# Loading the 4 KB rows of wq ahead of its 24 KB rows in a decode attention kernel

## The chip, the cores and the metric

The kernel runs on one core of a Trainium2 chip (trn2). The metric is the device time of one execution in microseconds (us). All times quoted are medians of runs that were marked fast; each run of a changed kernel was compared with runs of the kernel before on the same chip. "Span" is the length of the profiled execution, about 2 us shorter than the measured time. In lines of the profile PE is TensorE, PEld its weight loads, DVE VectorE, ACT ScalarE, POOL GpSimd and SP SyncE; a q behind such a name means the part of the engine that issues, q1 is SyncE's DMA queue, and L226 is line 226 of the kernel. A packet is the piece that a DMA engine moves at a time, here one row of wq.

## The reference

One token goes through grouped attention over a cache of 65536 keys and values, and through a small token mixer; a gate mixes the two. The code is shortened.

```python
x = A_x                                              # 1 x 1 x 448, bf16
g = _sigmoid((x * gate_w).sum(-1, keepdims=True))
# attention: 16 query heads of 256, 8 key/value heads, cache of 65536
q = (x @ wq)                                         # wq: 448 x 4096
scores = einsum("bhqd,bhkd->bhqk", q, k) * (256 ** -0.5)
a = (softmax(scores) @ v) @ wo                       # wo: 4096 x 448
# mixer: layernorm of x, then gelu(h * w1 + b1) @ w2 + b2, w1 and w2 of 1792
return g * a + (1 - g) * b
```

K and V are 268 MB each, wq and wo 3.67 MB each.

## The kernel before

SyncE issues all large loads on one queue. The matrix wq has 448 rows. The first 384 go to `wq_a`, three rows to a partition, so each of the 128 partitions takes 24 KB that lie side by side in memory. The last 64 rows go to `wq_b`, half a row (4 KB) to a partition. Both lie in the buffer `vbuf` that the V blocks use later, so the first V block may be loaded only when q has been computed.

```python
wq_a = early[:, 0:WF * NQ].rearrange("p (j n) -> p j n", j=WF)     # WF = 3, NQ = 4096; early is vbuf
wq_b = early[:, WF * NQ:WF * NQ + HALF]                            # HALF = 2048
...
@block.sync
def _(eng):
    eng.dma_start(wq_a.rearrange("p j n -> p (j n)"),
                  A_wq[0:WF * P, :].rearrange("(p j) n -> p (j n)", p=P)).then_inc(sem_wq, 16)
    eng.dma_start(wq_b, A_wq[WF * P:DM, :].rearrange("r (a n) -> (r a) n", a=2)
                  ).then_inc(sem_wq, 16)
    ...
    for j in range(NP):                          # 32 blocks of 8 MB of K and of V
        if j >= 1:
            eng.wait_ge(sem_tr[NB - 1], BODY * (j - 1) + DC)   # half of block j-1 transposed
        if j == 0:
            load(kring, A_k_cache, j, HV, NV, 0, sem_k)        # half a block: rows of 32 KB
            load(kring, A_k_cache, j, 0, HV, 0, sem_kb)
        ...
        if j == 0:
            eng.wait_ge(s_q, 1)                  # q is there, wq is used up
            eng.wait_ge(s_hb, 1)
        else:
            eng.wait_ge(sem_pv, j)               # V block j-1 is used up
        load(vbuf, A_v_cache, j, ...)            # rows of 64 KB
```

ScalarE issues the row x and five small loads besides (gate, w1, b1, w2, b2); TensorE waits for them, then for both loads of wq:

```python
pe.wait_ge(sem_misc, 16 * 5)
pe.matmul(acc[:, WF + 2:WF + 2 + 3 * FT], wrows_b, identb, ...).then_inc(s_col, 1)
pe.wait_ge(s_xcol, 1)            # VectorE has copied the columns of x out of acc
pe.wait_ge(sem_wq, 32)           # both loads of wq
# 128 matmuls of q: 3 from wq_a and 1 from wq_b for each column
```

The softmax here doesn't subtract the row's maximum and nothing guards it: scores larger than these inputs give would overflow.

## Time and profile before

| kernel before | |
|---|---|
| measured time | 1266.03 us (1266.0 to 1266.64, 3 runs) |
| profiled span | 1264.0 us |
| DMA bytes, mean rate | 544.39 MB, 431 GB/s |
| share of SyncE's queue (q1) | 99.7% |
| busiest compute engine | PE, 73% |
| last wq row landed / q started | 12.1 us / 12.59 us |
| first V block issued | 17.54 us |

Read it from the DMA side: 544 MB must be moved, SyncE's queue alone takes 99.7% of what the 16 DMA engines could give in the span, and no compute engine is busy more than 73% of it. The lines of the profile that carry this stand in the prediction below.

### The profile page before, as it was taken

The page shows a single profiled execution, that of the slowest core. Times are in us where ns is not written, and L with a number is a line of the kernel's source. Part 1 is how long each engine was busy: PE and PEld are TensorE (multiplying, and loading weights), DVE is VectorE, ACT ScalarE, POOL GpSimd, SP SyncE. Part 2 cuts the span into 40 slices and gives each one's busy share as a digit, 9 for nine tenths or more (in the row PEclk, how much of TensorE's full clock was granted, in tenths as well). Part 3 has the DMA queues.
Part 4 walks back from the last instruction along what each step waited for, and adds up shares of the span by engine and source line. Part 5 has one row for each costly group of instructions (what it writes and reads, how often), then busy time and mean ns, then how long its engine had stood idle before and what let it go on. Part 6 is the DMA issues. An engine that isn't in the chain of part 4 may idle for free.

```text
span 1264.0 us, 38850 instructions
## 1 busy us (share of the span) xinstructions
PE 917.0 (73%) x17114; PEld 868.4 (69%) x17114; DVE 422.5 (33%) x764; ACT 538.2 (43%) x788; POOL 0.9 (0%) x7
## 2 busy tenths in 40 slices
PE   3876678766778667786676876758767688676688
PEld 2766668766677666786666876658766578666687
DVE  2433344333444333443222332323322233332233
ACT  1443345533355433454333553335533355433455
POOL 0000000000000000000000000000000000000000
PEclk9887788787898887987888987889887888877999
DMA  9999999999999999999999999999999999999998
GB/s 411 428 434 436 433 431 431 431 438 431 433 433 433 433 431 438 425 433 440 431 436 429 431 431 433 440 433 433 431 431 431 438 436 433 431 433 431 431 427 367
DMA packets 11623, 544.39 MB, mean 431 GB/s; under 512 B 1369, under 2 KB 1628, under 8 KB 2908
## 3 DMA queue, kind: packets, MB, share of 16 engines
q1 hardware_dynamic: 11522, 544.22, 99.7%
q8 instruction: 8, 0.13, 0.0%
q10 hardware_dynamic: 90, 0.01, 0.0%
q14 instruction: 3, 0.02, 0.0%
HBM read 544.22 MB, written 0.00 MB: 431 GB/s over the span
## 4 chain that ended last, share of the span: by engine, by line
DMA 70%; PE 29%; issue 1%; SPq 0%; DVEq 0%; DVE 0%; ACT 0%; ACTq 0%
DMA kring<-in_A_k_cache_dram 68%; PE kst L298 24%; PE sps L318 4%; DMA wo_sb<-in_A_wo_dram 2%; PE acc L358 0%; SPq L231 0%; SPq L265 0%; SPq L228 0%; SPq L226 0%; PE prj L405 0%; PE acc L347 0%; DVEq L92 0%; DVE out_row L634 0%; ACT pT L658 0%; ACTq L658 0%
## 5 line engine op out<-in xcount | busy, mean ns | idle before, releaser
L298 PE MATMUL kst<-ident,kring 128*128 128x128 f32 x4096 | 563.7, 299 | 304.9 <-DMA kring<-in_A_k_cache_dram 294.1
L669 ACT ACTIVATE ktT<-kst 128x1024 bf16<-128x1024 bf16 x512 | 500.0, 1021 | 667.3 <-PE kst L298 666.5
L298 PEld LDWEIGHTS kst<-ident,kring 128*128 128x128 f32 x4096 | 514.0, 156 | 314.8 <-issue 312.2
L569 DVE COPY ktT<-kst 128x1024 bf16<-128x1024 bf16 x512 | 354.2, 692 | 765.0 <-PE kst L298 742.0
L318 PEld LDWEIGHTS sps<-qcur,ktT 128*128 128x128 bf16 x8192 | 237.8, 96 | 4.1 <-issue 1.6
L318 PE MATMUL sps<-qcur,ktT 128*128 128x2 bf16 x8192 | 236.6, 163 | 1.3 <-issue 1.3
L358 PE MATMUL acc<-vbuf,pT 128*2 128x256 bf16 x4080 | 140.4, 305 | 3.8 <-issue 3.3
L358 PEld LDWEIGHTS acc<-vbuf,pT 128*2 128x2 bf16 x4080 | 105.2, 93 | 30.6 <-issue 3.8
L658 ACT ACTIVATE pT<-sps 128x32 f32 x256 | 51.8, 202 | 16.4 <-PE sps L318 16.4
L347 PE MATMUL acc<-pT,ones_sq 128*128 128x32 bf16 x256 | 11.7, 178 | 12.3 <-ACT pT L658 12.3
L347 PEld LDWEIGHTS acc<-pT,ones_sq 128*128 128x128 bf16 x256 | 8.6, 96 | 15.2 <-ACT pT L658 14.9
L675 ACT ACTIVATE z_b<-z_b 128x448 bf16<-128x448 bf16 x14 | 8.1, 577 | 20.5 <-DVE z_b L556 20.4
L575 DVE COPY accs<-acc 128x288 f32<-128x288 f32 x8 | 3.7, 458 | 38.5 <-PE acc L358 38.5
L394 PEld LDWEIGHTS acc<-sel,accs 128*64 128x64 f32 x112 | 10.8, 214 | 0.9
L394 PE MATMUL acc<-sel,accs 128*64 128x1 f32 x112 | 11.4, 260 | 0.0
L431 PE MATMUL acc<-vbuf 42*128 42x42 bf16 x1 | 0.2, 214 | 8.3 <-DMA b_b<-in_B_b_dram 8.3
L405 PE MATMUL prj<-wo_sb,oTn 128*1 128x112 bf16 x128 | 3.7, 244 | 3.1 <-DVE oTn L600 2.9
L431 PEld LDWEIGHTS acc<-vbuf 42*128 42x128 bf16 x1 | 0.1, 102 | 8.4 <-DMA b_b<-in_B_b_dram 8.4
L562 DVE TENSOR_TENSOR gu<-wtmp,z_b 128x448 bf16<-128x448 bf16 x14 | 5.5, 393 | 1.0
L554 DVE TENSOR_TENSOR z_b<-u_b,wtmp 128x448 bf16<-128x448 bf16 x14 | 5.5, 393 | 1.0
L550 DVE TENSOR_TENSOR z_b<-wtmp,u_b 128x448 bf16<-128x448 bf16 x14 | 5.5, 393 | 1.0
L548 DVE TENSOR_TENSOR wtmp<-u_b 128x448 bf16<-128x448 bf16 x14 | 5.5, 392 | 1.1
(89 smaller groups left out, 82.5 us busy)
## 6 DMA issues: line engine op xcount, KB each, us to landing
kring<-in_A_k_cache_dram SPq DMA_DIRECT2D x4, 4096.0 KB, 24.3
vbuf<-in_A_v_cache_dram SPq DMA_DIRECT2D x1, 6144.0 KB, 25.7
wo_sb<-in_A_wo_dram SPq DMA_DIRECT2D x7, 448.0 KB, 27.6
vbuf<-in_A_wq_dram SPq DMA_DIRECT2D x1, 3072.0 KB, 10.2
vbuf<-in_A_v_cache_dram SPq DMA_DIRECT2D x1, 1024.0 KB, 27.8
vbuf<-in_A_v_cache_dram SPq DMA_DIRECT2D x1, 768.0 KB, 28.9
vbuf<-in_A_wq_dram SPq DMA_DIRECT2D x1, 512.0 KB, 10.9
vbuf<-in_A_v_cache_dram SPq DMA_DIRECT2D x31, 29.7
```

Source lines behind the costliest of these rows:

```text
L298: ins = pe.transpose(kst[:, b, i * P:(i + 1) * P], kring_f[:, at + NT * (k % DC) + 4 * b + i, :], ident[:, :])
L318: ins = pe.matmul(sps[:, par, 2 * nt:2 * nt + 2], ktT[:, par, b, ntl * DH + dj:(ntl + 1) * DH:2], qcur[:, dj, :], start=(dj == 0), stop=(d ...
L347: pe.matmul(acc[:, DENC:SELC], ones_sq[:, :], pT[:, r, :], start=False, stop=(r == BODY - 1), skip_group_check=True)
L358: ins = pe.matmul(acc[o:o + REP, 0:DH], pT[:, r, 2 * nt:2 * nt + 2], vbuf[:, n, :], start=False, stop=False, skip_group_check=True)
L394: ins = pe.matmul(dst[hh * HP:(hh + 1) * HP, i:i + 1], accs[:, i:DH:2 * REP], sel[:, hh:hh + 1], start=False, stop=True, skip_group_check= ...
L548: vec.tensor_tensor(W, U, U, op=ALU.mult)
L550: vec.tensor_tensor(Z, W, U, op=ALU.mult)
L554: vec.tensor_tensor(Z, U, W, op=ALU.add)
L569: vec.tensor_copy(ktT[:, k % KTB, b, :], kst_b[:, b, :]).then_inc(sem_ev[b], 1)
L658: act.activation(pT[:, bass.ds(p0 + k % DC, 1), :].rearrange("p o n -> p (o n)"), sps[:, k % 2, 0:2 * NT], AF.Exp, scale=scale).then_inc(s ...
L669: act.activation(ktT[:, k % KTB, b, :], kst_b[:, b, :], AF.Copy).then_inc(sem_ev[b], 1)
L675: act.activation(z_b[:, :], z_b[:, :], AF.Tanh).then_inc(s_tanh, 1)
```

## The change

The intent is to have the short rows ahead of the long ones. Two issues on SyncE change places; nothing else does.

```diff
         def _(eng):
+            eng.dma_start(wq_b, A_wq[WF * P:DM, :].rearrange("r (a n) -> (r a) n", a=2)
+                          ).then_inc(sem_wq, 16)
             eng.dma_start(wq_a.rearrange("p j n -> p (j n)"),
                           A_wq[0:WF * P, :].rearrange("(p j) n -> p (j n)", p=P)).then_inc(sem_wq, 16)
-            eng.dma_start(wq_b, A_wq[WF * P:DM, :].rearrange("r (a n) -> (r a) n", a=2)
-                          ).then_inc(sem_wq, 16)
```

## The prediction

> **What bounds the kernel now.** I read the page first, for the busy shares and the DMA lines:
>
> ```profile
> PE 917.0 (73%) x17114; PEld 868.4 (69%) x17114; DVE 422.5 (33%) x764; ACT 538.2 (43%) x788; POOL 0.9 (0%) x7
> DMA  9999999999999999999999999999999999999998
> GB/s 411 428 434 436 433 431 431 431 438 431 433 433 433 433 431 438 425 433 440 431 436 429 431 431 433 440 433 433 431 431 431 438 436 433 431 433 431 431 427 367
> q1 hardware_dynamic: 11522, 544.22, 99.7%
> HBM read 544.22 MB, written 0.00 MB: 431 GB/s over the span
> ```
>
> No compute engine is busy more than 73% of the span. The DMA row stands at 9 in all slices but the last, and the one queue that SyncE feeds, q1, fills 99.7% of what 16 engines could do. The bytes are all needed: K and V are 8 x 65536 x 256 x 2 bytes = 268.4 MB each, wq and wo 448 x 4096 x 2 = 3.67 MB each, together 544.2 MB, as the page counts. A table of windows gives 433 GB/s from 60 to 1200 us. 544.22 MB / 433 GB/s is 1256.8 us of the span of 1264.0, so 7.2 us are left for the start, the landing of the last bytes and the tail.
>
> The end comes next. The chain of waits from 1180 us on names the last link:
>
> ```profile
> 1232.11 29.33 DMA wo_sb<-in_A_wo_dram
> 1261.44 0.04 issue
> 1261.49 0.39 PE prj L405 x6
> 1261.87 0.02 issue
> 1261.90 0.26 DVE out_row L634
> 1262.16 0.30 DVEq L92
> ```
>
> The last load of wo is issued at 1232.11 and lands 29.33 us later although it is 0.23 MB: it stands in the queue behind the last piece of V. After it come 2.56 us of projection, copy and store. So the time is: first byte, plus all bytes at the queue's rate, plus a fixed tail, provided the queue never runs dry. (The measured 1266.03 us are about 2 us over the profiled span; I take that as constant.)
>
> Now the place that the change touches. The timeline of the first 40 us, SyncE's rows:
>
> ```profile
> 0.74 0.41 SPq L226 DMA_DIRECT2D vbuf<-in_A_wq_dram  x1
> 1.20 0.41 SPq L228 DMA_DIRECT2D vbuf<-in_A_wq_dram  x1
> 1.67 1.10 SPq L231 DMA_DIRECT2D kring<-in_A_k_cache_dram  x2
> ...
> 17.54 0.33 SPq L231 DMA_DIRECT2D vbuf<-in_A_v_cache_dram  x1
> 17.91 0.43 SPq L260 DMA_DIRECT2D wo_sb<-in_A_wo_dram  x1
> 38.79 0.33 SPq L231 DMA_DIRECT2D kring<-in_A_k_cache_dram  x1
> ```
>
> Both loads of wq are issued back to back, and both halves of the first K block directly behind. SyncE then waits until 17.54 us before it may issue the first V block, which overwrites the buffer that holds wq: it needs q. The timeline also tells what q needs (start, duration, instruction, then in brackets what ended the idle time):
>
> ```profile
> 11.08 0.21 PE L431 MATMUL acc<-vbuf 42*128 42x42 bf16 x1 [8.33 <-DMA b_b<-in_B_b_dram]
> 12.37 0.17 DVE L517 CAST xcol<-acc 128x5 bf16<-128x5 f32 x1
> 12.59 0.24 PE L441 MATMUL sps<-xcol,vbuf 128*128 128x1 bf16 x3 [1.30 <-DVE xcol L517]
> ```
>
> and the list of DMA issues gives the landing of each load of wq, in us from its issue, as the last column:
>
> ```profile
> vbuf<-in_A_wq_dram SPq DMA_DIRECT2D x1, 3072.0 KB, 10.2
> vbuf<-in_A_wq_dram SPq DMA_DIRECT2D x1, 512.0 KB, 10.9
> ```
>
> The 24 KB rows land at 0.74 + 10.2 = 10.9 us, the 4 KB rows at 1.20 + 10.9 = 12.1. TensorE starts q at 12.59, and what released it is not wq but xcol. That copy waits for a matmul which waited until 11.08 for the five small loads (gate, w1, b1, w2, b2) that ScalarE issues.
>
> **What the Trainium skill says.** "DMA: Bandwidth & Descriptors", section "Queues, rings and completion order": on each engine descriptors are consumed in ring order. The trace agrees: the second load of wq lands 12.1 - 10.9 = 1.2 us after the first, and its 0.524 MB at 431 GB/s are 1.22 us. The same page, "Why a DMA increments its semaphore by 16 and not by 1", says that only the full 16 of a load means its data are there. Here both loads count on one semaphore and TensorE waits for 32, the sum of the two, so their order gives no early start to any consumer. Its section "Where 436 GB/s comes from" puts the ceiling of the 16 ports at 435.2 GB/s; 433 in the middle of this trace is 99.5% of it, so no order of rows can raise the rate by more than half a per cent. "Issuing engines are not separate DMA queues" says that loads issued by ScalarE run on the same 16 engines and interleave with SyncE's: the last small load is issued at 2.79 us and its release is seen only at 11.05, some 8.3 us, when wq is nearly through. The trace agrees in that they share.
>
> **The change part by part.** Nothing is removed or added. The orders of all instructions on TensorE, VectorE, ScalarE and GpSimd are the same; on SyncE the first two DMA issues change places. Rows, sizes, destinations and semaphores stay.
>
> The issue: 0.41 us each (the timeline: 0.74 and 1.20), so K is issued at 1.67 as before. Cost 0.
>
> The landing: 24 KB rows, 3.146 MB / 431 GB/s = 7.30 us. Landing 10.2 us after issue, they show about 2.9 us of start, completion and sharing. The 4 KB rows, now first, should land at about 0.74 + 2.9 + 1.2 = 4.8 us (an estimate from these durations) instead of 12.1. The 24 KB rows move behind them, from 10.9 to about 12.1. The later of the two, which is what the wait for 32 sees, stays at 12.1. Gain 0.
>
> The small loads: with shorter packets in front when they enter, they may land earlier than 11.05. Then q starts when wq is there, at 12.1 rather than 12.59: at most 0.5 us, which moves the V issue from 17.54 to about 17.05. If they land later, V goes later by as much.
>
> What half a microsecond at the V issue is worth: wq and the first K block are 3.67 + 8.39 = 12.06 MB, 28.0 us at 431 GB/s; the first bytes move at about 1.75 us, so the queue holds work until about 29.7 us. V issued at 17.54 has 12.2 us to spare. The next link has slack too: the second K block is issued at 38.79, and with V (8.39 MB, 19.5 us) and wo (0.46 MB, 1.1 us) the queue lasts until 29.7 + 20.6 = 50.3, so 11.5 us to spare. In the steady part, one K block was issued at 629.43 while the V block issued at 607.67 needed, at the median of 29.7 us, until 637.4: 8 us. A shift of 0.5 us in any of these stays hidden. Sum: 0 + 0 + 0, from 1266.03 to about 1266.
>
> **The rivals.** (1) The swap brings q forward and the gain reaches the end. For it: q stands at the head of the chain that frees the V buffer. Against it: the slack of 12.2 us behind it. Even if it went through undiminished, it would be 0.5 us, 1265.5. (2) The small loads are starved instead: their turn comes after more of the queue. For it: they already take 8.3 us. They could be 12.2 us later without cost. Should they come only after the whole first K block, near 30 us, then by the 6.5 us that now lie between 11.05 and the V issue, V would be issued near 36.5, the queue would be dry for about 7 us, and the time 1273, still within 0.6%. (3) The first load runs out before the second is ready, as it is now only 0.524 MB. Its bytes last 1.22 us; the second issue follows 0.46 us behind. A gap, if any, is some tenths: 1266.3. (4) TensorE bounds the steady part, its clock being granted at 0.84; then nothing at the start matters either. SyncE's 643.4 us of waits on the transposes look like this, but they are spent with the queue full, as the 99.7% shows. Again 1266.
>
> **Range and chances.** All paths but (2) lie within 1 us of 1266.0. The three runs before span 0.64 us, and another session may differ by about as much again, so the range is 1265.0 to 1267.2, with 1266.1 as the value. A gain of 2% would be 25 us, three times all that the kernel spends beyond its bytes (7.2 us of span); I give it 0.005. A loss of 2% needs a dry queue of 25 us, more than three times rival (2): 0.01.
>
> **What would show it.** In the changed profile the load of 512 KB lands about 4 us after its issue and that of 3072 KB about 11 us after its own, both near 4.8 and 12.1 us of the span; q starts between 12.1 and 12.8; V is issued between 17 and 18; q1 stays at 99.7%; the last load of wo lands within 1 us of 1261.4. The prediction is wrong if the V issue falls after 29 us, if the DMA row shows a slice below 9 ahead of the end, or if the middle rate leaves 433 GB/s by more than 1: each GB/s there is 2.9 us.

## The result, and the profile after

The changed kernel took 1265.59 us (1265.48 to 1267.19, 6 runs), the kernel before 1266.1 us (1265.96 to 1266.64, 6 runs). The ratio is 0.9997, with a 95% interval of 0.9984 to 1.001: the same, by the criterion of 2%. (A ratio here is the mean time of one kernel's fast runs over that of the other's of the same rounds, so it is not quite the ratio of the medians.) Still, five of the six new runs lie between 1265.48 and 1265.69, below every run of before (the sixth, 1267.19, lies above them all). So a second question is worth asking: are about 0.5 us really gained, and where?

The page of the changed kernel first; the queue is as full, and the bytes are the same:

```profile
DMA  9999999999999999999999999999999999999998
q1 hardware_dynamic: 11522, 544.22, 99.7%
HBM read 544.22 MB, written 0.00 MB: 431 GB/s over the span
```

The windows table gives 433 GB/s from 60 to 1200 us, as before. Next the list of DMA issues of the changed kernel (last column: us from issue to landing), then two lines of its timeline (start, duration, instruction, and in brackets what ended the idle time before it):

```profile
vbuf<-in_A_wq_dram SPq DMA_DIRECT2D x1, 3072.0 KB, 10.3
vbuf<-in_A_wq_dram SPq DMA_DIRECT2D x1, 512.0 KB, 3.4
```

```profile
11.54 0.21 PE L431 MATMUL acc<-vbuf 42*128 42x42 bf16 x1 [8.79 <-DMA b_b<-in_B_b_dram]
13.05 0.24 PE L441 MATMUL sps<-xcol,vbuf 128*128 128x1 bf16 x3 [1.30 <-DVE xcol L517]
...
18.00 0.33 SPq L231 DMA_DIRECT2D vbuf<-in_A_v_cache_dram  x1
```

The 4 KB rows land at 0.74 + 3.4 = 4.1 us and the 24 KB rows at 1.20 + 10.3 = 11.5, so wq is complete 0.6 us sooner than the 12.1 of before. But q starts later, at 13.05 instead of 12.59, because the small loads release TensorE at 11.54 instead of 11.08; V is issued at 18.00 instead of 17.54. Whatever was gained was not gained through q.

Then the chain of waits, which follows the K loads (start, duration in us). Before:

```profile
1.67 21.40 DMA kring<-in_A_k_cache_dram
...
38.79 34.06 DMA kring<-in_A_k_cache_dram
```

After:

```profile
1.67 21.05 DMA kring<-in_A_k_cache_dram
...
38.84 33.48 DMA kring<-in_A_k_cache_dram
...
1232.02 28.92 DMA wo_sb<-in_A_wo_dram
```

The first half of K lands at 22.72 instead of 23.07 us, the second K block at 72.32 instead of 72.85, the last load of wo at 1260.94 instead of 1261.44. The lead is 0.35, then 0.53, then 0.50 us: most of it is there when the first half of K has landed, and from the second K block on it stays. The step from 0.35 to 0.53 is not placed by these lines. The packets show the start as well. In the window from 1.5 to 3.3 us of the kernel before, the queue's line reads

```profile
q1 hardware_dynamic: 16, 0.39, 91.5%
```

that is, 16 packets (the first of each engine) took 0.915 x 1.8 us x 16 / 16 = 1.65 us each, while from 4.4 to 9 us a 24 KB packet takes 0.91 us by the same reckoning. So the first packet of each engine costs about 0.7 us more than a later one. After the change the same window holds

```profile
q1 hardware_dynamic: 113, 0.46, 76.2%
```

113 packets of 0.19 us, some seven for each engine, where a 4 KB packet in mid-stream takes 0.16 us (the same reckoning in a window of the run e2_k_half_first): about 0.25 us too much in all.

### The profile page after: what moved, and what is told of

It reads as the page before. It is cut to its first block, busy times and chain, and to the rows that moved or that the text cites. A ratio compares the mean times of both kernels' runs of the same rounds, so it can differ in the third digit from the quotient of the medians.

```text
span 1263.4 us, 38848 instructions
## 1 busy us (share of the span) xinstructions
PE 917.3 (73%) x17112; PEld 867.5 (69%) x17114; DVE 422.4 (33%) x764; ACT 537.9 (43%) x788; POOL 0.9 (0%) x7
## 3 DMA queue, kind: packets, MB, share of 16 engines
q1 hardware_dynamic: 11522, 544.22, 99.7%
## 4 chain that ended last, share of the span: by engine, by line
DMA 70%; PE 29%; issue 1%; SPq 0%; DVEq 0%; DVE 0%; ACT 0%; ACTq 0%
DMA kring<-in_A_k_cache_dram 68%; PE kst L298 24%; PE sps L318 4%; DMA wo_sb<-in_A_wo_dram 2%; PE acc L358 0%; SPq L231 0%; SPq L265 0%; SPq L228 0%; SPq L226 0%; PE acc L347 0%; DVEq L92 0%; PE prj L405 0%; DVE out_row L634 0%; ACT pT L658 0%; ACTq L658 0%
## 5 line engine op out<-in xcount | busy, mean ns | idle before, releaser
L347 PE MATMUL acc<-pT,ones_sq 128*128 128x32 bf16 x256 | 11.6, 178 | 12.2 <-ACT pT L658 12.2
## 6 DMA issues: line engine op xcount, KB each, us to landing
vbuf<-in_A_wq_dram SPq DMA_DIRECT2D x1, 3072.0 KB, 10.3
```

Of the source, the lines that this page charges most:

```text
L347: pe.matmul(acc[:, DENC:SELC], ones_sq[:, :], pT[:, r, :], start=False, stop=(r == BODY - 1), skip_group_check=True)
```

## The experiments

Twelve kernels ran, in three groups of four. The median of before was 1266.15 us in the first group (9 runs), 1266.0 in the second (9) and 1266.23 in the third (9). First the theories. In all of them, "the start" is the time until the DMA engines move data at their full pace. A: the 4 KB packets themselves make the start quicker. B: short rows cost less in front than between longer rows. C: the small loads of ScalarE share the engines differently. N: it is noise. D, formed after the first two groups: what counts is how the rows of the first load lie in memory, with their starts close together (4 or 8 KB apart) or 24 KB apart. In the kernel before they lie side by side too, but as each is 24 KB long, their starts are 24 KB apart. Beside D, A is called A2 below (only the length of the first packets counts), and L is a rival by which the address of the first load counts.

### Is the gain real?

e1_after_again is the changed kernel once more.

> The changed kernel once more, to see whether its 0.5 us are there at all. Theory A (the first packet of each DMA engine is 4 KB instead of 24 KB, so the engines get going sooner, and all later landings move forward by a constant): 0.4 to 0.6 us below the kernel before, with the last load of wo landing about 0.5 us earlier. Rival N (noise, nothing moved): the difference is under 0.2 us or changes sign between rounds.

Measured: 1265.6 us (1265.44 to 1265.97, 5 runs), 0.55 below before; the last wo landed at 1261.01 us, 0.4 earlier. Three of the five runs lie below all nine of before, the other two (1265.84 and 1265.97) below eight of them. The gain is there, at 0.04% of the time. (The 95% interval for the ratio, 0.9982 to 1.001, is too wide to tell it from 1; the claim rests on the order of the runs, on its return in a second set of runs, and on the landings.)

### Is it the length of the first packets, or the place of the short rows?

e2_k_half_first puts rows of 32 KB in front:

```diff
+            load(kring, A_k_cache, 0, HV, NV, 0, sem_k)     # then wq_a, wq_b, other half of K
```

> The first half of the first K block (rows of 32 KB) goes ahead of both loads of wq, which keep the order of before. Theory A: the first packet is 8 KB longer than before, so 0.1 to 0.3 us over the kernel before. Rival B (4 KB rows between 24 KB and 32 KB rows cost time, the start does not matter): equal to before within 0.1 us, since the 4 KB rows still stand between larger ones. Both: q comes about 9.7 us later, V is issued near 27.3 us, still ahead of the end of the queue near 29.7, so nothing else is lost.

Measured: 1268.04 us (1267.38 to 1269.44), 1.9 us over before, which neither theory allowed for. The loss lies elsewhere (below). The start itself speaks against A: wq was complete at 1.67 + 19.7 = 21.4 us, while the order of before would give about 12.1 + 4.19 MB / 431 GB/s = 21.8 with a half of K added. In e5 below, whose 24 KB rows come first and which has moved the same bytes by then, wq was complete at 1.67 + 20.4 = 22.1.

e3_three_8k loads the 24 KB rows as three loads of 8 KB rows that lie 24 KB apart:

```diff
+            wq_r = A_wq[0:WF * P, :].rearrange("(p j) n -> p (j n)", p=P)
+            for i in range(WF):
+                eng.dma_start(wq_a.rearrange("p j n -> p (j n)")[:, i * NQ:(i + 1) * NQ],
+                              wq_r[:, i * NQ:(i + 1) * NQ]).then_inc(sem_wq, 16)
-            pe.wait_ge(sem_wq, 32)
+            pe.wait_ge(sem_wq, 64)
```

> The 24 KB rows are loaded as three loads of 8 KB rows, then the 4 KB rows last, as before. Theory A: the first packet is 8 KB, so about 0.4 us below before (16/20 of 0.5), less what two more loads cost (their issue of 0.4 us each lies behind 1.05 MB of queued work, so about nothing). Rival B: no gain, 0 to 0.4 us over before, since there are more short rows between longer ones.

Measured: 1266.04 us (1265.79 to 1266.2), 0.1 below before, where A gave 0.4. This run shows something else of use. Its small loads landed much sooner, and V was issued 0.5 us earlier than before (timeline):

```profile
8.47 0.38 DVE L513 TENSOR_TENSOR vbuf<-vbuf 1x448 bf16<-1x448 bf16 x1 [2.51 <-DMA b_b<-in_B_b_dram]
...
17.04 0.33 SPq L233 DMA_DIRECT2D vbuf<-in_A_v_cache_dram  x1
```

An earlier V issue by itself therefore bought at most 0.1 us. That is the prediction's rival 1, tried.

e4_4k_of_24k_first loads the first 4 KB of each 24 KB row, then the other 20 KB, then the 4 KB rows of the remainder:

```diff
+            for n0, n1 in ((0, HALF), (HALF, WF * NQ)):
+                eng.dma_start(wq_a.rearrange("p j n -> p (j n)")[:, n0:n1],
+                              wq_r[:, n0:n1]).then_inc(sem_wq, 16)
```

> The first 4 KB of each 24 KB row are loaded first, then the other 20 KB, then the 4 KB rows of the remainder last, as before. Theory A: as the changed kernel, 0.4 to 0.6 us below before, although the 4 KB rows of the remainder stand where they stood. Rival B: equal to before within 0.1 us.

Measured: 1266.17 us (1266.11 to 1266.52), equal to before. Theory A falls: short packets in front are not enough. B, which had named this result, still stood.

### How much slack is there behind q?

Both runs leave the 24 KB rows first and move the issue of `wq_b`: in e5_4k_between_k between the halves of the first K block, in e6_4k_after_k behind both.

```diff
             if j == 0:
                 load(kring, A_k_cache, j, HV, NV, 0, sem_k)
+                eng.dma_start(wq_b, ...).then_inc(sem_wq, 16)      # e5
                 load(kring, A_k_cache, j, 0, HV, 0, sem_kb)
+                eng.dma_start(wq_b, ...).then_inc(sem_wq, 16)      # e6, in place of the other
```

> The 4 KB rows are loaded between the two halves of the first K block, to measure the slack that the prediction worked out. wq is complete only near 24 us, q some 5 us before V can be issued, so V is issued near 29. Slack theory (queue lasts until about 29.7 us): between 1266.0 and 1267.5 us, as the first byte of V comes about 1 us after its issue. Rival (slack much smaller than worked out, a late V costs at once): 5 us or more over before.

> The 4 KB rows are loaded after both halves of the first K block: wq is complete near 32 us, V issued near 37 us, while the queue ends near 31 us. Slack theory: the queue is dry for 6 to 8 us, and that comes out whole at the end, 1272 to 1274 us. Rival (the loss is made up later, as TensorE has time to spare): under 1269 us.

Measured: e5 1269.37 us (1268.24 to 1270.56), 3.4 over before; e6 1275.94 us (1275.56 to 1277.76), 9.9 over. V was issued at 27.12 and 36.67 us. In e6 the direction of the slack theory held, though 1275.94 lies above the 1272 to 1274 it named. The windows table has 360 GB/s from 25 to 31 us and 118 from 31 to 40; against 433 that is about 1.0 + 6.5 = 7.5 us missed, and nothing was made up later. A second, smaller gap comes at the second V block (issued at 78.41): 410 and 395 GB/s from 70 to 80 and from 80 to 90 us, another 1.4 us. In e5 the theory failed, as it had in e2 (and the rival's 5 us or more did not come either): V came well ahead of the end of the queue, and yet time was lost. The timeline and the windows table show where (its columns are the window, its length, the busy time of PE, PEld, DVE, ACT and POOL, the granted clock, the DMA share and GB/s). First e5:

```profile
49.36 0.33 SPq L229 DMA_DIRECT2D kring<-in_A_k_cache_dram  x1
73.95 0.33 SPq L229 DMA_DIRECT2D vbuf<-in_A_v_cache_dram  x1
```

```profile
70.00:80.00 10.00, 9.13 (x148) 7.25 (x141) 2.77 (x4) 3.82 (x5) 0.00 (x0) 0.82 0.64 246
```

and before:

```profile
63.58 0.33 SPq L231 DMA_DIRECT2D vbuf<-in_A_v_cache_dram  x1
```

```profile
70.00:80.00 10.00, 7.03 (x71) 7.02 (x72) 2.82 (x5) 4.08 (x5) 0.00 (x0) 0.66 1.01 434
```

In the windows lines, look at the last figure: 246 GB/s in e5 against 434 in before, for the same ten microseconds. The load that comes too late is the second V block, not the first. It waits for TensorE to have used up the first block (`sem_pv`), and TensorE could begin on that block only after q. It was issued at 73.95 us, 10.4 us later than in before, when the second K block was about to land (49.36 + 25.48 = 74.84). The dry stretch is 10 us x (1 - 246/433) = 4.3 us, and the span of this run is 1268.3 - 1264.0 = 4.3 us longer. In e2 the second V block came at 70.92, 7.3 us later than in before, and the span is 1.9 us longer. On the line through these two points the loss starts when the second V block is issued about 5 us late. That is an estimate, from two runs, and a rough one: without any loss this issue came at 60.84 us in the changed kernel and at 63.58 in before.

### Do the small loads make the difference?

In both twins ScalarE issues the small loads only after wq has landed; e7_before_small_late has the order of before, e8_after_small_late that of after.

```diff
+            act.wait_ge(sem_wq, 32)
             act.dma_start(grow_b, gate_w.rearrange("(a n) -> a n", a=1)).then_inc(sem_misc, 16)
```

> Order of before, but ScalarE issues its five small loads only when wq has landed, so their 88 packets no longer interleave with those of wq. Theory A: the start is as before, wq lands near 12 us, the time is that of before within 0.2 us as long as V is issued ahead of about 29 us. Rival C (the gain of the change came from the small packets, which shared the engines with 24 KB packets in another way): 0.3 to 0.6 us below before, or no difference left between this run and its twin with the order of after.

> Order of after, with the five small loads held back until wq has landed, as in the twin run with the order of before. Theory A: 0.4 to 0.6 us below the twin. Rival C: within 0.1 us of the twin.

Measured: e7 1272.64 us (1271.45 to 1275.35), e8 1272.07 us (1271.2 to 1274.35). Both are 6 us over before, because behind K's 32 KB rows the small loads took far longer than I had allowed for. In the chain of e7 they are the link

```profile
13.52 12.74 DMA b_b<-in_B_b_dram
```

and V was issued only at 32.76. The medians of the twins differ by 0.57 us, as A said and C did not; but the runs of each spread over 3 us, so this alone is weak. Firmer is the landing of wq, ahead of any of the five small loads; in the chains of e7 and e8 it is

```profile
1.20 10.82 DMA vbuf<-in_A_wq_dram
```

```profile
1.20 10.30 DMA vbuf<-in_A_wq_dram
```

that is, 12.0 us in e7 and 11.5 in e8. The 0.5 us are there without the small loads. C falls.

### Is it how the rows of the first load lie in memory?

Two twins of the changed kernel differ from it only in what the first load reads (the result is then wrong; sizes, counts and order stay). In e10_after_pitch_24k the 4 KB rows lie 24 KB apart; in e12_after_first_rows they lie side by side, but at the start of wq instead of its end.

```diff
+            eng.dma_start(wq_b, wq_r[:, 0:HALF]).then_inc(sem_wq, 16)                      # e10
+            eng.dma_start(wq_b, A_wq[0:DM - WF * P, :].rearrange("r (a n) -> (r a) n", a=2)
+                          ).then_inc(sem_wq, 16)                                           # e12
-            eng.dma_start(wq_b, A_wq[WF * P:DM, :].rearrange("r (a n) -> (r a) n", a=2)
-                          ).then_inc(sem_wq, 16)
```

> The changed kernel with the same sizes, counts and order, but the 4 KB rows are read from the first 4 KB of each 24 KB row, so 24 KB apart; the result is wrong on purpose. Theory D: the gain is gone, 1266.0 to 1266.3 beside 1266.1 of before. Theory A2, and theory B (short rows cost less in front than in the middle): the gain stays, 0.4 to 0.6 us below before.

> The changed kernel, with its first load reading the first 64 rows of wq instead of the last 64, contiguous as they are; the result is wrong on purpose. Theory D: the gain stays, 0.4 to 0.6 us below before. Rival L (it is where in memory the first load reads, not how its rows lie): the gain is gone.

Measured: e10 1266.07 us (1266.04 to 1266.12), 0.16 below the before of its group; e12 1265.59 us (1265.41 to 1266.0), 0.64 below. Between the twins lie 0.48 us, and their ranges do not overlap: the slowest run of e12, 1266.0, still lies below all of e10's. The list of DMA issues gives the landing of the first load, us from its issue, e10 first:

```profile
vbuf<-in_A_wq_dram SPq DMA_DIRECT2D x1, 512.0 KB, 3.9
```

```profile
vbuf<-in_A_wq_dram SPq DMA_DIRECT2D x1, 512.0 KB, 3.3
```

The traces of the other runs with a first load of 4 KB rows say the same: 3.4 us in after, e1 and e11 and 3.3 in e8, where the rows lie side by side, and 4.0 in e4, where they lie 24 KB apart. The chain gives the landing of the second K block, e10 first:

```profile
38.61 34.21 DMA kring<-in_A_k_cache_dram
```

```profile
38.68 33.82 DMA kring<-in_A_k_cache_dram
```

72.82 and 72.50 us, against 72.85 in before. So with the same packet lengths in the same order, most of the gain goes when the rows of the first load lie 24 KB apart. B, which had the place of the short rows as the cause, falls with e10. The address as such (rival L) falls with e12, as far as addresses within wq go. Both twins read some rows of wq twice; e4, which has the first load of e10 and reads nothing twice, lost the gain as well.

If D were the whole rule, two more kernels should have gained. e9_8k_contiguous (correct result) is e3 with each of its three loads reading one contiguous megabyte:

```diff
+            for i in range(WF):
+                eng.dma_start(wq_a[:, i, :], A_wq[i * P:(i + 1) * P, :]).then_inc(sem_wq, 16)
-                pe.matmul(acc[:, j:j + 1], xrow_b[0:1, j:WF * P:WF], one, start=True, stop=True)
+                pe.matmul(acc[:, j:j + 1], xrow_b[0:1, j * P:(j + 1) * P], one, start=True, stop=True)
```

> The big part of wq is loaded as three loads of 128 rows of 8 KB, each load from one contiguous megabyte, ahead of the 4 KB rows. Only the source order differs from the run with three loads of 8 KB that lay 24 KB apart, which gained 0.1 us. Theory D (the start is slow where the first load's rows lie 24 KB apart over 3 MB, and quick where they lie side by side): 0.3 to 0.6 us below before, wq complete about 0.3 us sooner. Theory A2 (what counts is the length of the first packets only): as that run, 0.1 us below before. Correct result.

e11_e4_contiguous (wrong result) is e4 with a contiguous first load:

```diff
+            eng.dma_start(wq_a.rearrange("p j n -> p (j n)")[:, 0:HALF],
+                          A_wq[WF * P:DM, :].rearrange("r (a n) -> (r a) n", a=2)).then_inc(sem_wq, 16)
+            eng.dma_start(wq_a.rearrange("p j n -> p (j n)")[:, HALF:WF * NQ],
+                          wq_r[:, HALF:WF * NQ]).then_inc(sem_wq, 16)
```

> The run with a 4 KB load in front, the other 20 KB and the 4 KB rows last, which gained nothing, but its first load reads the contiguous half megabyte of the remainder rows in place of rows 24 KB apart; the result is wrong on purpose. Theory D: now 0.3 to 0.6 us below before. Theory B: still equal to before within 0.15 us, as 4 KB rows still stand last.

Measured: e9 1265.86 us (1265.83 to 1265.93), 0.37 below before, within what D expected; but wq was complete at 2.13 + 9.8 = 11.9 us as in e3, not 0.3 us sooner, and its first megabyte landed 5.0 us after its issue in both (the list of DMA issues for the first window). So its trace does not show where its 0.37 us come from. e11 1266.05 us (1265.88 to 1266.31), 0.18 below, not the 0.3 to 0.6 of D; its second K block landed at 37.75 + 35.12 = 72.87, no sooner than in before. Its first load landed as soon as that of the changed kernel (3.4 us), so the start was gained and lost again. The load behind it shows where: in the window from 4.4 to 9 us only its 20 KB packets start on the queue, in e11 first and then in e4

```profile
q1 hardware_dynamic: 88, 1.80, 100.2%
```

```profile
q1 hardware_dynamic: 96, 1.97, 99.7%
```

that is 0.84 us for a packet in e11 and 0.76 in e4, the same rows of wq in both. At eight packets for each engine the difference is about 0.6 us, as much as the first load had gained.

So D is half a rule. For a first load of 4 KB rows, the spacing decides over 0.5 us of its landing and, where nothing else differs (e10 against e12), over the time. It is not shown for longer rows: e9 and e3 land their first load alike, and in e2 the rows of 32 KB begin 64 KB apart, yet wq was complete sooner than in e5. And what is gained can be lost in the next load (e11). Why the start of before is slow, with rows that lie side by side, and what in the memory or the engines makes the difference, stays open.

### All runs at one glance

| run | first load (row length, spacing) | us | against before | second K block landed |
|---|---|---|---|---|
| before | 24 KB, contiguous over 3 MB | 1266.0 to 1266.23 | | 72.85 |
| after / e1_after_again | 4 KB, contiguous | 1265.59 / 1265.6 | -0.5 / -0.55 | 72.32 / 72.39 |
| e12_after_first_rows | 4 KB, contiguous, other place | 1265.59 | -0.64 | 72.50 |
| e9_8k_contiguous | 8 KB, contiguous | 1265.86 | -0.37 | 72.69 |
| e10_after_pitch_24k | 4 KB, 24 KB apart | 1266.07 | -0.16 | 72.82 |
| e3_three_8k | 8 KB, 24 KB apart | 1266.04 | -0.1 | 72.78 |
| e11_e4_contiguous | 4 KB, contiguous; then 20 KB, 24 KB apart | 1266.05 | -0.18 | 72.87 |
| e4_4k_of_24k_first | 4 KB, 24 KB apart | 1266.17 | 0.0 | 73.08 |
| e2, e5, e6 | wq later | 1268.04, 1269.37, 1275.94 | +1.9, +3.4, +9.9 | |
| e7, e8 | small loads later | 1272.64, 1272.07 | +6.6, +6.1 | |

No version beat the changed kernel by more than the runs spread: e12 computes a wrong result, and e9 is slower. The median of before itself moves by 0.23 us from group to group, so differences of that size between groups say nothing; e9 to e12 share one group.

## Why the prediction was right

The time (1266.1 predicted, 1265.59 measured) and its main reason hold, and three of its steps do not.

- **The queue sets the time: held.** The share of 99.7%, the 433 GB/s in the middle and the bytes are unchanged. e6 shows the other side: what the queue misses, here nearly 10 us, comes out at the end.
- **The landing: "The later of the two ... stays at 12.1. Gain 0." Wrong by a little.** wq was complete at 11.5 us. The term missing in the sum was the start: the prediction took it as one sum of 2.9 us of start, completion and sharing that does not depend on which load is first. With the 4 KB rows in front this part measured 3.4 - 1.2 = 2.2 us, and they landed at 4.1, not 4.8. The lead stays: 0.35 us when the first half of K lands, 0.5 us at the second K block and at the end. e10 against e12 shows that what the first load reads decides over it; the mechanism is open. The sum 0 + 0 + 0 should have been about -0.5. The value, 1266.1, was high by that much; the range held it.
- **The small loads: "with shorter packets in front when they enter, they may land earlier." Wrong in sign.** They came 0.46 us later, so q started at 13.05 instead of between 12.1 and 12.8, and V at 18.00, the edge of what was named. The likely reason, not tested by itself, is that the short packets were used up too soon: the 4 KB rows had landed at 4.1 us, while the last small load was issued at 2.77 and waited beside 24 KB rows from then on. Where short packets do stand in front while they wait (8 KB in e3) they landed 2.6 us sooner.
- **The slack of 12.2 us behind the V issue: too large.** A V issue 8.9 us later (e2) already cost 1.9 us. The prediction looked at the first V block and at K, and took the slack of later links from their issues in the kernel before, as if a late q did not move them. A late q delays TensorE's first block, and through it the second V block, where the room is some 5 us by the estimate above. At the first V issue the true slack lies between 0.9 us (e10, V at 18.44, as fast as before) and 8.9. That the conclusion stood is in part luck: q moved the other way than forecast, and only because the shift was 0.5 us did neither error show.
- **The rivals.** (1) q brought forward was tried by e3: V 0.5 us earlier, at most 0.1 us gained. The 1265.5 it would have brought is close to the 1265.59 measured, but the half microsecond came another way, with q later. (2) Starved small loads did not come about through the change. e7 and e8 brought them about, with V near 32.6 us and 6 us lost; e6, with V at 36.67, lost 9.9, where the prediction had put about 7 for V at 36.5. The dry stretch that it worked out is there, some 7.5 us; what it lacked is above all the second gap, at the second V block. (3) A gap behind a short first load did not show as a loss: the changed kernel was faster. (4) TensorE as the bound of the steady part: the queue stayed at 99.7%, and nothing spoke for it.

## What to carry to other kernels

Where one DMA queue is full from start to end, and no wait behind it comes late, the order of two loads at its head can save little, here 0.5 of 1266 us; look for time in the bytes, or in places where the queue runs dry. When you work out the slack of a wait, follow the delay on to the next loads that depend on it, and see which of them comes late first: here it was the second V block, not the one whose wait was looked at. Small loads on another queue can land late beside long rows: here they were released some 8.3 us after the last issue beside 24 KB rows, 5.5 beside 8 KB rows (e3) and 12.7 behind 32 KB rows (e7). That cost 6 us in e7, where V came late by it; where the wait had slack, landing sooner gained at most 0.1 us (e3).

## What the Trainium skill lacked or had wrong

- "DMA: Bandwidth & Descriptors", section "Latency and other measured facts", gives a first-byte latency and notes the effect of row pitches that are large powers of two. It has nothing on a start that depends on how the rows of the first load lie at a pitch like 24 KB: two kernels alike in all packet lengths and in order differed by 0.48 us (e10 1266.07, e12 1265.59), their first loads landing 3.9 and 3.3 us after issue. Nor does it say that the first packets of a run are slow: those of 24 KB took 1.65 us where later ones took 0.91.
- The same page says in "Queues, rings and completion order" that an engine takes turns between queues by packets. It gives no measure of what this does to small loads beside a full queue. Here the last of five small loads was issued at 2.79 us and released its consumers at 11.05 us beside 24 KB rows; in e3 it was issued at 2.98 and released them at 8.47 beside 8 KB rows; behind 32 KB rows the chain has 12.74 us for it (e7).
